# Beacon attention and a two-layer MLP in one kernel: the first sequence cut at query 240, up weights loaded in quarters

## The chip, the cores and the metric

The kernel runs on one core of a Trainium2 chip. The metric is the device time of one execution in microseconds (us), lower is better. The engines are named as in the profile: PE multiplies matrices (PEld loads its weights), ACT (ScalarE) and DVE (VectorE) work on tiles in on-chip memory, POOL (GpSimd) too, and SP issues DMAs; ACT and POOL issue DMAs as well.

## The reference

Eight sequences of 576 tokens, 8 heads of 64 each, with 16 beacon keys and values in front that every query sees:

```python
scores = scale * np.matmul(q, k_all.transpose(0, 1, 3, 2))
causal[:, Nb:] = np.triu(np.ones((S, S), dtype=bool), k=1)
scores = np.where(causal, -1000000000.0, scores)
a = np.exp(scores - scores.max(-1, keepdims=True))
a /= a.sum(-1, keepdims=True) + 1e-09
attn_out = np.matmul(a, v_all)
x = attn_out.transpose(0, 2, 1, 3).reshape(B * S, H * D)
h = x @ w_in
out = np.maximum(0.01 * h, h) @ w_out
```

q, k and v are 8 x 8 x 576 x 64, w_in is 512 x 2048, w_out 2048 x 512, and out 4608 x 512, all float32.

## The kernel before

**Units.** A group is one pair of heads of one sequence; sequence b has groups 4b to 4b+3, so there are 32. Tokens go through the MLP in 9 chunks of 512. Matmuls take bfloat16.

**Attention of one group.** Keys lie along partitions in five blocks (128, 128, 128, 128, 80 rows, the first with the 16 beacon keys). `score` multiplies key blocks with queries into a PSUM tile of two heads x 512 columns (two such buffers), and ACT takes the exponential of the whole tile into `aT` (line 276 in the first eight groups, 329 and 333 later). POOL then zeroes the triangles above the diagonal (`triangle`, line 289). `value` multiplies `aT` with the values, which carry a column of ones, in two halves (query tiles 0 to 2, then 3 and 4; line 359); DVE takes the reciprocal of the row sums (388) and multiplies (389). For groups 0 to 3 PE turns the result and DVE or ACT copies it into `xT` (405, 410).

**The MLP.** An up block (`moe1`, run by `up`) is 4 matmuls of 128 x 512 (line 442) for one of 16 slices of the hidden width, and a Prelu on ACT (450). It needs the tokens of all four groups of a sequence. Chunk 0 goes down through plain matmuls (`moe2_plain`, line 519, 16 down blocks); later chunks use sums of weights and of tokens to save products (line 544).

**Order.** The program is scheduled by hand: every engine runs its instructions in the order in which the code issues them. The prologue is written as strings of steps for `run` (lines 927 to 938): s scores, m masks, v values, q and k turn a group's queries and keys, x finishes a group, u an up block, d a down block, l and V and N load, i and o load up and down weights, w and W are matmuls on a blank tile whose result nothing reads. The prologue computes groups 0 to 7, chunk 0's up blocks and its first down blocks; from group 8 on a list of events with due times fills in up and down blocks between scores and values.

**Loads.** All loads of q, k, v and weights are issued by POOL and cast from float32 on the way, except for the keys of group 0, which SP loads as float32 and ACT and DVE cast (928, 929). Loads for groups 0 to 7 put 9 consecutive rows of a head in one partition (`load_qk`, 158), and PE turns them (`t_q`, 243; copies at 249). Up weights come in two halves (131), down weights in two halves (137).

## Time and profile before

| what | value |
|---|---|
| median of 3 runs | 324.78 us (323.4 to 324.84) |
| span of the profiled execution | 323.8 us |
| PE busy | 314.3 us (97%), 3468 matmuls |
| ACT, DVE, POOL busy | 203.8, 168.0, 184.3 us |
| first exponential | 7.74 us |
| first up matmul | 26.07 us |
| scores of sequence 2 begin | 61.15 us |

The records give one profiled execution, known by its span from the first to the last instruction; the median of the runs is 1.0 us above it. PE's busy time counts pipelined matmuls with their latency, so a busy PE need not be at its peak: an up matmul is recorded as 379 ns long while 537 of them keep PE busy for 116.5 us, 217 ns each. In the first 18 us part of PE's busy time is matmuls on the blank tile.

### The profile page before, as it was taken

What the parts mean: (1) busy time and instruction counts of PE and PEld (TensorE: products, weight loads), DVE (VectorE), ACT (ScalarE), POOL (GpSimd) and SP (SyncE); (2) the same over time, 40 slices, a digit from 0 to 9 for tenths busy, and PEclk for the clock granted to TensorE, in tenths of its full rate; (3) what the DMA queues carried; (4) which work ended last, traced back from release to release, by engine and by line L of the source; (5) the groups of instructions that cost most, each with busy time, mean ns of one, the idle gap of its engine ahead of it and who ended that gap; (6) DMA issues with size and microseconds to landing.
All of it is one profiled execution on the core that took longest, in us unless ns stands there. A gap on an engine that the chain in (4) does not pass through costs nothing.

```text
span 323.8 us, 8701 instructions
## 1 busy us (share of the span) xinstructions
PE 314.3 (97%) x3468; PEld 219.1 (68%) x3494; DVE 168.0 (52%) x341; ACT 203.8 (63%) x346; POOL 184.3 (57%) x354
## 2 busy tenths in 40 slices
PE   7999999999999999999999999999999999999995
PEld 4575555444588557855788888656875697688784
DVE  3464245508255244444443454525464689577954
ACT  4968962387855786478746874687458547455510
POOL 8895868999996787659875977666221000000000
PEclk9999999999999999999999999999999999999999
DMA  8999999999999999999999999999222100200123
GB/s 137 129 189 192 124 214 140 169 177 188 135 152 160 216 138 129 114 186 97 141 176 174 99 143 119 188 128 129 44 81 82 26 2 32 75 25 2 65 67 130
DMA packets 155256, 39.78 MB, mean 123 GB/s; under 512 B 142368, under 2 KB 152480, under 8 KB 155216
## 3 DMA queue, kind: packets, MB, share of 16 engines
q0 software_dynamic: 99824, 18.54, 91.1%
q1 hardware_dynamic: 55120, 20.62, 38.3%
q8 instruction: 27, 0.44, 0.6%
q14 instruction: 13, 0.11, 0.1%
q10 hardware_dynamic: 272, 0.07, 0.1%
HBM read 37.22 MB, written 9.44 MB: 144 GB/s over the span
## 4 chain that ended last, share of the span: by engine, by line
PE 72%; DMA 14%; POOL 9%; ACT 3%; issue 1%; DVE 0%; POOLq 0%; ACTq 0%; SPq 0%
PE acc L442 24%; PE acc L544 19%; PE sc L544 11%; PE av L359 6%; PE sc L314 5%; PE acc L663 5%; DMA w_out_sb<-in_moe_w_out_dram 4%; DMA gsum<-in_k_dram 4%; POOL aT L289 3%; DMA k_nat<-in_k_dram 3%; DMA v_aug<-in_v_dram 2%; ACT aT L333 2%; DMA kT<-k_nat 2%; POOL gsum L158 1%; POOL v_aug L214 1%
## 5 line engine op out<-in xcount | busy, mean ns | idle before, releaser
L442 PE MATMUL acc<-xT,w_in_sb 128*128 128x512 bf16 (+1 forms) x537 | 116.5, 354 | 1.5 <-ACT aT L329 0.3
L450 ACT ACTIVATE gT<-acc 128x512 bf16<-128x512 f32 x124 | 70.8, 623 | 33.1 <-PE acc L442 32.6
L289 POOL TENSOR_SCALAR_AFFINE_SELECT aT<-aT 128x256 bf16<-128x256 bf16 (+2 forms) x160 | 59.7, 403 | 51.4 <-ACT aT L329 31.5
L442 PEld LDWEIGHTS <-w_in_sb 128*128 128x128 bf16 x560 | 51.7, 98 | 43.9 <-issue 2.9
L544 PEld LDWEIGHTS <-gT 128*128 128x128 bf16 x512 | 48.7, 98 | 7.7 <-issue 1.8
L333 ACT ACTIVATE aT<-sc 128x1024 bf16<-128x1024 f32 (+3 forms) x64 | 51.7, 892 | 0.0
L329 ACT ACTIVATE aT<-sc 128x512 bf16<-128x512 f32 (+3 forms) x64 | 29.0, 520 | 27.8 <-PE sc L314 27.8
L388 DVE RECIPROCAL rec<-av 128x6 f32<-128x6 f32 (+1 forms) x64 | 12.0, 187 | 65.0 <-PE av L359 64.4
L359 PEld LDWEIGHTS <-aT 128*128 128x128 bf16 (+1 forms) x960 | 36.9, 98 | 9.2 <-issue 1.4
L544 PEld LDWEIGHTS <-gsum 128*128 128x128 bf16 x384 | 36.5, 98 | 6.5 <-issue 0.4
L359 PE MATMUL av<-v_aug,aT 128*128 128x65 bf16 (+1 forms) x960 | 39.8, 194 | 0.8 <-DMA v_aug<-in_v_dram 0.4
L214 POOL DMA_DIRECT2D v_aug<-in_v_dram x40 | 34.1, 856 | 4.2 <-DMA w_in_sb<-in_moe_w_in_dram 3.8
L171 POOL DMA_DIRECT2D k_nat<-in_k_dram x48 | 34.8, 730 | 0.9 <-DMA w_out_sb<-in_moe_w_out_dram 0.3
L171 POOL DMA_DIRECT2D q_nat<-in_q_dram x48 | 34.8, 729 | 0.6 <-issue 0.4
L389 DVE TENSOR_TENSOR x_nat<-av,rec 128x384 bf16<-128x384 f32 (+1 forms) x64 | 31.4, 491 | 2.2
L544 PE MATMUL acc<-w_out_sb,gT 128*128 128x256 bf16 x240 | 28.9, 273 | 0.4 <-ACT gT L450 0.4
L276 ACT ACTIVATE aT<-sc 128x1024 bf16<-128x1024 f32 (+3 forms) x32 | 26.0, 874 | 4.7 <-PE sc L267 2.5
L314 PE MATMUL sc<-qT,kT 64*128 64x80 bf16 (+22 forms) x384 | 22.2, 250 | 0.3
L314 PEld LDWEIGHTS <-kT 64*128 64x128 bf16 x384 | 12.8, 94 | 11.2 <-issue 7.6
L544 PE MATMUL acc<-w_sum,gsum 128*128 128x256 bf16 x160 | 20.1, 273 | 0.0
L575 ACT COPY p<-acc 128x512 f32<-128x512 f32 x15 | 9.1, 604 | 16.8 <-PE acc L544 16.8
L785 DVE TENSOR_TENSOR gsum<-gT 128x1024 bf16<-128x1024 bf16 x16 | 11.0, 688 | 15.7 <-ACT gT L450 15.7
(95 smaller groups left out, 339.0 us busy)
## 6 DMA issues: line engine op xcount, KB each, us to landing
out_dram<-p SPq DMA_DIRECT2D x26, 256.0 KB, 3.2
q_nat<-in_q_dram POOLq DMA_DIRECT2D x48, 72.0 KB, 5.5
k_nat<-in_k_dram POOLq DMA_DIRECT2D x48, 72.0 KB, 5.3
v_aug<-in_v_dram POOLq DMA_DIRECT2D x24, 128.0 KB, 6.5
w_in_sb<-in_moe_w_in_dram POOLq DMA_DIRECT2D x2, 1024.0 KB, 12.4
w_out_sb<-in_moe_w_out_dram POOLq DMA_DIRECT2D x2, 1024.0 KB, 12.1
out_dram<-u SPq DMA_DIRECT2D x8, 256.0 KB, 2.7
gsum<-in_q_dram POOLq DMA_DIRECT2D x8, 144.0 KB, 7.1
```

The lines of the kernel that those rows point to most:

```text
L171: nc.gpsimd.dma_start(out=t[:, :, par], in_=(q, k)[which][b, 2 * hp + par].rearrange("(t p) d -> p t d", p=NR),)
L214: nc.gpsimd.dma_start(out=dst[lo : ROWS[c], c, :, 0:D], in_=v[b, :, OFF[c] : OFF[c] + n].rearrange("h p d -> p h d"),)
L276: nc.scalar.activation(out=aT[:, :, c0 : c0 + w], in_=sc[:, :, 0:w], func=AF.Exp, scale=0.125)
L289: nc.gpsimd.affine_select(out=view, in_=view, compare_op=ALU.is_ge, fill=0.0, base=128 - n if lo == 0 else 0, channel_multiplier=-1, patte ...
L314: nc.tensor.matmul(out=(sc[par] if apart else sc[:, par])[:, at : at + b - a], lhsT=kT[ps_, c * 128 : (c + 1) * 128], rhs=qT[ps_, q0 : q0 ...
L329: nc.scalar.activation(out=probs[g][:, par, lo:hi], in_=sc[par][:, at : at + hi - lo], func=AF.Exp, scale=0.125)
L333: nc.scalar.activation(out=probs[g][:, :, lo:hi], in_=sc[:, :, at : at + hi - lo], func=AF.Exp, scale=0.125)
L359: nc.tensor.matmul(out=avv[:, n, 0 : D + 1], lhsT=aT[0 : ROWS[c], par, a0 : a0 + 128], rhs=va[0 : ROWS[c], c, 2 * hp + par, :], start=(c = ...
L389: nc.vector.tensor_tensor(out=x_nat[:, t0:t1].rearrange("p t e d -> p (t e) d"), in0=avv[:, :, 0:D], in1=rec[:, n0:n1, None].to_broadcast( ...
L442: nc.tensor.matmul(out=acc[:, lo:hi], lhsT=w_in_cols(fc, j), rhs=xT[:, j, x0 : x0 + hi - lo], start=(j == 0), stop=(j == NJ - 1), skip_gro ...
L450: nc.scalar.activation(out=gT[i][:, fc, :], in_=acc, func=AF.Prelu, alpha=0.01)
L544: nc.tensor.matmul(out=acc[:, lo : lo + HD], lhsT=left(i, n, fc, tile), rhs=right(n, fc), start=(lo == 0 and fc == 0), stop=(fc == HF - 1) ...
```

## The change

Sequence 0 (groups 0 to 3) is taken in two parts. Part a is queries 0 to 239 against the first two key blocks; part b is queries 240 to 575 against all five.

- Rows 0 to 255 of q and k of the four groups come in eight float32 loads (`load_a`), keys on SP's queue and queries on ACT's; ACT, DVE and POOL cast them for two groups at a time (`cast_a`), PE turns two groups with 8 transposes, and four copies put them in place (`turn_a`). Rows 256 to 575 come in eight casting loads on POOL (`load_b`) and are turned by `turn_b`, four copies of 320 columns for each two groups.
- `score_a` puts a group's part a in one tile of 368 columns a head; `score_b` puts part b in three tiles (512, 512, 272 columns).
- The masks of part a of groups 0 and 1 are multiplications with a triangle of ones on DVE (`mask_a`); the others stay on POOL.
- `value` is cut after query tile 1; the turn into `xT` is cut there too.
- `moe1_early` computes two of the 16 slices of chunk 0 for tokens 0 to 239 and takes them through one Prelu; tokens 240 to 511 follow in `moe1`, 272 columns wide. The early half of eight slices stands inside part b, that of the other eight among the scores of group 5.
- Up weights come in four loads.
- The blank matmuls are 9 at the start; the other 50 are taken out.

The new order on ACT. Before, from the third score tile of group 2 (`aT2`) to the first up block; `gT` is the hidden layer:

```order
L276 ACTIVATE aT2_92<-sc_409 128x2x416
L276 ACTIVATE aT2_92<-sc_458 128x2x288
L276 ACTIVATE aT3_93<-sc_472 128x2x512
L276 ACTIVATE aT3_93<-sc_494 128x2x464
L276 ACTIVATE aT3_93<-sc_518 128x2x416
L276 ACTIVATE aT3_93<-sc_551 128x2x288
L410 COPY xT_86<-tp_557 128x576
L249 COPY kT_94<-tp_635 128x576
L410 COPY xT_86<-tp_693 128x576
L276 ACTIVATE aT0_90<-sc_700 128x2x512
L276 ACTIVATE aT0_90<-sc_704 128x2x464
L450 ACTIVATE gT_721<-acc_722 128x512
```

Now, from the part a exponential of group 2; L346 is part a, L369 part b, L549 the Prelu of `moe1_early`, L509 the copy into `xT`:

```order
L346 ACTIVATE aT2_93<-sc_211 128x2x368
L346 ACTIVATE aT3_94<-sc_228 128x2x368
L369 ACTIVATE aT0_91<-sc_287 128x2x512
L509 COPY xT_87<-tp_315 128x240
L369 ACTIVATE aT0_91<-sc_319 128x2x512
L509 COPY xT_87<-tp_327 128x240
L549 ACTIVATE gT_334<-acc_335 128x2x240
L369 ACTIVATE aT0_91<-sc_345 128x2x272
L549 ACTIVATE gT_334<-acc_352 128x2x240
L369 ACTIVATE aT1_92<-sc_363 128x2x512
L369 ACTIVATE aT1_92<-sc_397 128x2x512
L369 ACTIVATE aT1_92<-sc_406 128x2x272
```

The first Prelu stood behind all exponentials of groups 0 to 3 and two of group 4; now it stands between the second and the third part b exponential of group 0.

The new order on DVE, ahead of the first up matmuls. Before, the casts and copies that turn keys and queries (`k_nat`, `tp`), then the first values:

```order
L929 CAST k_nat0_97<-gsum2_96 64x9x64
L249 COPY kT_94<-tp_202 128x117
L249 COPY kT_94<-tp_202 128x459
L249 COPY qT_230<-tp_231 128x576
L249 COPY kT_94<-tp_259 128x576
L249 COPY qT_295<-tp_296 128x576
L249 COPY kT_94<-tp_320 128x576
L249 COPY qT_386<-tp_387 128x576
L249 COPY kT_94<-tp_415 128x576
L388 RECIPROCAL rec_441<-av_362 128x6
```

Now, from the triangle masks of group 1 (L377); L483 and L484 normalise values, L223 copies part b's keys and queries:

```order
L377 TENSOR_TENSOR aT1_92<-aT1_92,tri_81 128x2x112
L377 TENSOR_TENSOR aT1_92<-aT1_92,tri_81 128x2x128
L483 RECIPROCAL rec_218<-av_219 128x4
L484 TENSOR_TENSOR x_nat_217<-av_219,rec_218 128x256
L483 RECIPROCAL rec_235<-av_236 128x4
L484 TENSOR_TENSOR x_nat_234<-av_236,rec_235 128x256
L509 COPY xT_87<-tp_245 128x240
L223 COPY kT_95<-tp_257 128x320 x2
L223 COPY qT_171<-tp_270 128x320
L223 COPY qT_174<-tp_270 128x320
L509 COPY xT_87<-tp_283 128x240
L483 RECIPROCAL rec_294<-av_295 128x4
```

The masks, the normalisation of groups 0 and 1 and a copy into `xT` now stand ahead of the copies that part b's scores need.

The new order on POOL around the down weights. Before, from the masks of group 4 (`aT0`); `bk_raw` are the beacon keys:

```order
L289 AFFINE_SELECT aT0_90<-aT0_90 128x2x128 x3
L289 AFFINE_SELECT aT0_90<-aT0_90 80x2x80
L137 DMA w_out_sb_84<-in_moe_w_out_dram 128x4x1024
L185 DMA bk_raw_98<-in_beacon_k_dram 128x6x64
L289 AFFINE_SELECT aT1_91<-aT1_91 128x2x112
L289 AFFINE_SELECT aT1_91<-aT1_91 128x2x128 x3
L289 AFFINE_SELECT aT1_91<-aT1_91 80x2x80
L137 DMA w_out_sb_84<-in_moe_w_out_dram 128x4x1024
L289 AFFINE_SELECT aT2_92<-aT2_92 128x2x112
L171 DMA q_nat_963<-in_q_dram 96x6x64 x2
```

Now, from the last values of sequence 1; `aT2` and `aT3` belong to groups 6 and 7:

```order
L275 DMA v_aug1_90<-in_v_dram 128x8x64 x3
L275 DMA v_aug1_90<-in_v_dram 80x8x64
L396 AFFINE_SELECT aT2_93<-aT2_93 128x2x112
L150 DMA w_out_sb_85<-in_moe_w_out_dram 128x4x1024
L396 AFFINE_SELECT aT2_93<-aT2_93 128x2x128 x3
L396 AFFINE_SELECT aT2_93<-aT2_93 80x2x80
L246 DMA bk_raw_100<-in_beacon_k_dram 128x6x64
L396 AFFINE_SELECT aT3_94<-aT3_94 128x2x112
L150 DMA w_out_sb_85<-in_moe_w_out_dram 128x4x1024
L396 AFFINE_SELECT aT3_94<-aT3_94 128x2x128 x3
```

The two loads of down weights moved from behind the masks of groups 4 and 5 to behind the first masks of groups 6 and 7.

The diff, cut to its core:

```diff
+    QA, RA, RB = 240, 4, 5
+    LATE0 = 368
+    LATE = [0, 336, 672, 1008, 1216, 1296]
...
     def load_w_in(i):
-        n = DF // 2
-        loaded["w_in", i] = nc.gpsimd.dma_start(
-            out=w_in_sb[i], in_=w_in_r[:, :, i * n : (i + 1) * n]
+        n = DF // 4
+        half, at = i // 2, i % 2 * n
+        nc.gpsimd.dma_start(
+            out=w_in_sb[half][:, :, at : at + n], in_=w_in_r[:, :, i * n : (i + 1) * n]
         )
...
+    def load_a(g, which, eng):
+        _, hp, grp, rows = where(g)
+        eng.dma_start(
+            out=raw_a[grp][rows, which],
+            in_=(q, k)[which][0, 2 * hp : 2 * hp + 2, 0 : RA * RP].rearrange("h (p i) d -> p h i d", i=RA),
+        )
...
+    def turn_a(grp, copies):
+        n, w = RA * RP, RA * 128
+        ps = ps_one.tile([128, 1024], BF16, name="tp", tag="one")
...
+        for e in range(2):
+            for which in (1, 0):
+                copies[which * 2 + e](
+                    out=operand(2 * grp + e, which)[:, 0:n].rearrange("c (p i) -> c p i", i=RA),
+                    in_=ps[:, which * w : (which + 1) * w].rearrange("c (i e p) -> c e p i", i=RA, e=2)[:, e],
+                )
...
+    def score_a(g):
+        qT, kT = qk[g]
+        aT = probs[g] = a_bufs[g % NA]
+        sc = ps_sc.tile([128, 2, 512], FP32, name="sc", tag="sc")
+        for c in range(2):
+            w = QA - OFF[c]
...
+        nc.scalar.activation(
+            out=aT[:, :, 0:LATE0], in_=sc[:, :, 0:LATE0], func=AF.Exp, scale=0.125
+        )
...
+    def score_b(g, n):
+        qT, kT = qk[g]
+        lo, hi = n * 512, min(LATE[NKB], n * 512 + 512)
...
+        nc.scalar.activation(
+            out=probs[g][:, :, LATE0 + lo : LATE0 + hi], in_=sc[:, :, 0 : hi - lo], func=AF.Exp, scale=0.125
+        )
...
+    def mask_a(g, eng):
+        for lo, n in ((0, 112), (QA, 128)):
+            if eng == 0:
+                view = probs[g][:, :, lo : lo + n]
+                nc.vector.tensor_tensor(
+                    out=view, in0=view, in1=tri[:, None, 128 - n :].to_broadcast([128, 2, n]), op=ALU.mult
+                )
+            else:
+                triangle(probs[g], lo, n, 128)
...
+    def moe1_early(n):
+        if 0 not in gT:
+            gT[0] = gpool.tile([128, NF, 512], BF16, name="gT")
+        acc = ps_one.tile([128, 512], FP32, name="acc", tag="one")
+        for f in range(2):
+            moe1_part(acc[:, f * QA :], 2 * n + f, 0, QA, first=f == 0)
+        nc.scalar.activation(
+            out=gT[0][:, 2 * n : 2 * n + 2, 0:QA],
+            in_=acc[:, 0 : 2 * QA].rearrange("p (f t) -> p f t", f=2),
+            func=AF.Prelu,
+            alpha=0.01,
+        )
...
+        if i == 0:
+            moe1_part(acc, fc, QA, 512)
+            nc.scalar.activation(out=gT[0][:, fc, QA:], in_=acc[:, 0 : 512 - QA], func=AF.Prelu, alpha=0.01)
+            return
...
-        load_first_keys()
+        for g in range(NPAIR):
+            load_a(g, 1, nc.sync)
+        load_a(0, 0, nc.scalar)
         load_beacon_k(0, 2, nc.scalar)
+        for g in range(1, NPAIR):
+            load_a(g, 0, nc.scalar)
...
-        unused(13, 256)
+        unused(9, 256)
...
-        run("q0.1 k0 w2.384 s0.0 m0.0 w3.256 s0.1 q1 s0.2 m0.1 k1 s0.3 m0.2")
...
+        run("g0.1.1 g0.0.0 A0.0.0.1.1 a0 a1 g1.1.2 g1.0.0 j0.0 A1.0.0.1.0 j1.0 a2 f0.0 a3 f1.0 z0.0.0 j2.1 j3.1 L2.0 L2.1 L3.0 L3.1 B0.0.0.0.0 z1.0.0 b0.0 f2.0 f3.0 z2.1.0 b0.1 z3.1.0")
...
```

In the new strings g casts part a, A and B turn parts a and b, a and b score them, j and n mask them, f takes values, z turns a part into `xT`, c runs `moe1_early` and L loads part b.

210 lines of the change are left out of this document (140 added, 70 removed).

## The prediction

> **What bounds the kernel now.** I read the page first, then PE's waits by stretch, then the timeline of the first 62 us, then the groups by form there. The page:
>
> ```profile
> span 323.8 us, 8701 instructions
> ...
> PEclk9999999999999999999999999999999999999999
> ```
>
> The waits of the tensor engine (PE) from 61 us, where the scores of sequence 2 begin, to the end (us in total, times, longest):
>
> ```profile
> PE acc L544 <- ACT gT L450: 0.4, 2, 0.2
> PE acc L442 <- ACT aT L329: 0.3, 1, 0.3
> PE acc L519 <- issue: 0.2, 1, 0.2
> PE av L359 <- ACT gT L450: 0.2, 1, 0.2
> ```
>
> They are 1.1 us of 263: from there PE is the limit, and what it still has to do is the same before and after. So the change is worth what it does to the moment at which PE has the prologue behind it. The prologue in order of time (start, duration, engine, work, idle time before it):
>
> ```profile
> 0.81 1.21 SPq L165 DMA_DIRECT2D gsum<-in_k_dram  x2
> ...
> 1.07 2.95 PE L825 MATMUL av<-blank 128*128 128x256 bf16 x13 [1.07 <-DVE blank L917]
> ...
> 3.77 0.67 ACT L928 CAST k_nat<-gsum 64x576 bf16<-64x576 f32 x1 [0.28 <-DMA gsum<-in_k_dram]
> ...
> 5.62 0.74 DVE L929 CAST k_nat<-gsum 64x576 bf16<-64x576 f32 x1 [0.87 <-DMA gsum<-in_k_dram]
> ...
> 5.91 0.47 PE L243 MATMUL tp<-ident,gsum 64*64 64x64 bf16 x18 [0.83 <-DMA gsum<-in_q_dram]
> ...
> 7.31 0.39 PE L267 MATMUL sc<-qT,kT 64*128 64x512 bf16 x2
> ...
> 7.74 8.89 ACT L276 ACTIVATE aT<-sc 128x1024 bf16<-128x1024 f32 x11 [0.68 <-PE sc L267]
> ...
> 20.56 1.54 ACT L276 ACTIVATE aT<-sc 128x832 bf16<-128x832 f32 x2 [0.42 <-PE sc L267]
> ...
> 26.07 1.90 PE L442 MATMUL acc<-xT,w_in_sb 128*128 128x512 bf16 x7
> ```
>
> From 7.74 to 22.1 us ScalarE (ACT) runs the exponentials of the first four groups almost without a gap; PE looks busy then because blank matmuls fill it. The first up matmul starts at 26.07, when the four groups stand in xT. I call that moment T.
>
> **The change part by part.** Means by form in the first 62 us (behind the bar: busy us, mean ns, idle us):
>
> ```profile
> L450 ACT ACTIVATE gT<-acc 128x512 bf16<-128x512 f32 x16 | 9.2, 606 | 3.2 <-PE acc L442 2.8 <-PE tp L243 0.2
> ...
> L276 ACT ACTIVATE aT<-sc 128x1024 bf16<-128x1024 f32 x8 | 8.2, 1023 | 1.0 <-PE sc L267 1.0
> ...
> L276 ACT ACTIVATE aT<-sc 128x576 bf16<-128x576 f32 x8 | 5.3, 662 | 1.1 <-PE sc L267 1.0
> ...
> L389 DVE TENSOR_TENSOR x_nat<-av,rec 128x384 bf16<-128x384 f32 x8 | 4.5, 557 | 0.3
> ...
> L389 DVE TENSOR_TENSOR x_nat<-av,rec 128x256 bf16<-128x256 f32 x8 | 3.4, 424 | 0.3
> ...
> L410 DVE COPY xT<-tp 128x576 bf16<-128x576 bf16 x5 | 2.3, 455 | 3.8 <-PE tp L405 3.8
> ...
> L388 DVE RECIPROCAL rec<-av 128x4 f32<-128x4 f32 x8 | 1.4, 179 | 2.7 <-PE av L359 2.7
> ...
> L410 ACT COPY xT<-tp 128x576 bf16<-128x576 bf16 x2 | 1.3, 636 | 0.7 <-PE tp L405 0.7
> ...
> L249 DVE COPY kT<-tp 128x459 bf16<-128x459 bf16 x1 | 0.6, 625 | 0.0
> ...
> L249 DVE COPY kT<-tp 128x117 bf16<-128x117 bf16 x1 | 0.3, 283 | 0.6 <-PE tp L238 0.6
> ```
>
> And from the page, over the whole run:
>
> ```profile
> L289 POOL TENSOR_SCALAR_AFFINE_SELECT aT<-aT 128x256 bf16<-128x256 bf16 (+2 forms) x160 | 59.7, 403 | 51.4 <-ACT aT L329 31.5
> ...
> L276 ACT ACTIVATE aT<-sc 128x1024 bf16<-128x1024 f32 (+3 forms) x32 | 26.0, 874 | 4.7 <-PE sc L267 2.5
> ...
> L785 DVE TENSOR_TENSOR gsum<-gT 128x1024 bf16<-128x1024 bf16 x16 | 11.0, 688 | 15.7 <-ACT gT L450 15.7
> ```
>
> *Start.* The first 256 rows of q and k of all four groups now come in eight loads on SP's and ACT's queues. DVE and ACT can cast the first pair of groups once two key and two query loads have landed. Before, one load was cast at 3.77 and the next at 5.62; I take 5.2, nearer the later one, because the second query load stands third on ACT's queue; bounds 3.8 and 6.6. A cast takes .66 (744 ns x 512/576), eight transposes about .45 (18 small ones took .47), a DVE copy of 256 columns .42 (1.0 ns a column between the two L249 rows), the scores .45 with the hand-over (.39 and a gap). First exponential at 7.2, against 7.74.
>
> The Trainium skill ("DMA: Bandwidth & Descriptors", section "Issuing engines are not separate DMA queues") says that loads issued from different engines run on the same 16 DMA engines and that several issuers save issue time alone. By it the start would lie at the late bound, 1.4 us more. Two loads issued .6 apart here (0.81, two in 1.21) were cast 1.85 apart, which agrees.
>
> *ACT's work.* An exponential costs .81 ns a column and .2 fixed (from 1023 and 662 ns). Part a is 4 x 736 columns at .79, part b 4 x (1.02 + 1.02 + .64): 13.9 us, as much as now (16 x 874 ns = 14.0). New in this stretch are four Prelus of 480 columns at .58 (from 606 ns), one key copy and two xT copies at about .4 each (from 636 ns): 17.4 us in all, so 24.6 if ACT never idles.
>
> *ACT's new idle time.* First, part b of group 0 needs its q and k turned, and those copies stand on DVE behind all of part a: two casts 1.3, five copies 2.1, four masks by the new triangle 1.1 (at L785's .67 ns a column, 240 of 480 columns each pair and a fixed part; at most 2), two normalisations 1.2 (179 + 424 each), one xT copy .25, then three of the four 320-column copies at .49: 7.4 us from 5.2, so 12.6, and with the scores 13.1. ACT is through part a at 10.8, thus 2.3 idle; behind the waiting exponential stand the xT copies of groups 2 and 3, on which the first up matmuls wait. Second, those matmuls (c0) need the first 240 tokens of all four groups. DVE still has one copy, one xT copy and two normalisations (1.94, so 14.6); ACT copies the last xT piece after its next exponential, until 16.1; eight matmuls take 1.1 with their drain, and c0's Prelu stands ahead of the next exponential on ACT, as c0 stands ahead of its scores on PE: 1.3 idle. Together 3.6; bounds 0 (two score buffers cover it) and 5.5. The last exponential ends at 28.2.
>
> *Tail.* Two masks on GpSimd .8, the last value matmuls .4, DVE .74 (557 + about 180), transposes .35, copy .3: 2.6. T is 30.8, 4.7 later than 26.1. Before, 4.0 us lay between the last exponential and T, but PE turned and scored group 4 in them, which is priced next.
>
> *What is credited.* PE's prices, the first two from the groups, the others from the timeline:
>
> ```profile
> L442 PE MATMUL acc<-xT,w_in_sb 128*128 128x512 bf16 (+1 forms) x537 | 116.5, 354 | 1.5 <-ACT aT L329 0.3
> ...
> L544 PE MATMUL acc<-w_out_sb,gT 128*128 128x256 bf16 x240 | 28.9, 273 | 0.4 <-ACT gT L450 0.4
> ```
>
> ```profile
> 25.16 0.59 PE L267 MATMUL sc<-qT,kT 64*128 64x512 bf16 x4
> ...
> 27.90 0.48 PE L267 MATMUL sc<-qT,kT 64*128 64x336 bf16 x8
> 28.30 0.75 PE L243 MATMUL tp<-ident,gsum 64*64 64x64 bf16 x36
> ```
>
> 512 columns take 217 ns (116.5/537), 256 take 120 (28.9/240): halves cost more than a whole. By that slope 240 take about 115 and 272 about 128, so cutting chunk 0 adds 64 x 26 ns = 1.7 us to PE, .4 of it before T. Done before T: 8 of 16 blocks of 240 tokens, worth 32 x 217 x 240/512 = 3.25 us. Moved behind T: q and k of group 4 and two score tiles, .75 + .59 less their drains, 1.0. After T ACT has six Prelus at .41 and four exponentials for group 4, 6.0 us; PE has six blocks at .51 and .75 + 1.07, 4.9: 1.1 lost. Sum -3.25 + 1.3 + 1.0 + 1.1 = about +.1. The blank matmuls taken out (all but 9) lay in PE's idle time: nothing.
>
> *Loads.* On GpSimd the down weights go out behind the masks of groups 6 and 7 instead of 4 and 5, and part b of groups 2 and 3 behind masks that wait for ACT's fourth exponential.
>
> ```profile
> 39.96 0.77 POOL L137 DMA_DIRECT2D w_out_sb<-in_moe_w_out_dram  x1
> ...
> 53.70 3.61 PE L519 MATMUL acc<-w_out_sb,gT 128*128 128x512 bf16 x15
> ...
> 61.15 0.85 PE L314 MATMUL sc<-qT,kT 64*128 64x512 bf16 x12
> ```
>
> ```profile
> DMA to landing us min/median/max: 10.6/12.1/13.7
> ```
>
> The second half (39.96) landed 13.7 later and PE started on it at 53.70. Now it is issued near 52, and PE reaches it near 58. If it lands in 6 us, because less is queued ahead, nothing is lost; that is taken. At the shortest landing shown, 10.6, it costs about 4, in the range. The up weights in quarters let c0 start on a quarter of the bytes; their landing is hidden behind the DVE chain, and if it were not, c0 alone would wait.
>
> **Sum.** 4.7 + .1 = 4.8 on the profiled span of 323.8, so 328.6. The median of the runs shown, 324.78, lies 1.0 above that span, so the forecast is 329.5.
>
> **Rivals.** *Dense start (faster).* Part a lands at 3.8, the first exponential starts at 5.8, ACT never idles, the tail shrinks to 1.9: T = 25.1, 1.0 earlier, and group 4 is no longer ACT's (1.1): -2.0 with the .1, 322.7. For it: the blanks show how little PE has to do there, and two score buffers cover short waits. Against it: the 7.4 us on DVE alone. With the other terms as summed it decides from T below 24.4.
>
> *Loads decide (same).* PE met the down weights as they landed (53.7). If the bytes pace the prologue, both kernels reach sequence 2 together: 324.8. For it: that meeting. Against it: PE's own work fills 26 to 61.
>
> *Down weights late (slower still).* The same chain plus 3.5: 333.0. It decides if the second half lands more than 6 us after its issue.
>
> *Cold PE (slower still).* The 13 blank matmuls at the start took 2.95 us, 227 ns for 256 columns against 120 later, so PE begins at half pace. With blanks gone from 3 to 17 us, the chained transposes, scores, values and c0, c1 could run so: 2 us of them doubled, 331.5. Against it: the granted clock reads 9 in every slice of the page and shows no such state.
>
> The Trainium skill ("TensorE: Matmul & The Clock Gate", Part 1) says that PE's clock is halved until about 3.4 us of sustained matmuls and again after an idle window, and its Part 4 that transposes don't count as activity. By it this rival would hold, at 331.5.
>
> **How the numbers follow.** A measurement of this kernel tells about 0.5% (1.6 us) from no change. Forecast .52 (its own range 327 to 332.5), dense start .16, loads decide .14, down weights late .10, cold PE .08. So slower .52 + .10 + .08 = .70, same .14, faster .16. The range takes in dense start and late weights with a later start: 322.5 to 334.0.
>
> **What would show it.** In the changed kernel's timeline: first exponential near 7.2; ACT idle about 2 us after the fourth 736-column exponential, ended by scores that wait for a DVE copy; c0 near 16.1; the first 272-column matmul near 31; PE's waits for the down weights under 1 us; first scores of sequence 2 near 67, with two more down blocks done. Wrong would be T below 27, or PE with fewer idle gaps before T than now, or a join that waits for loads.

## The result, and the profile after

The changed kernel takes 350.31 us in the median of 4 runs (348.82 to 350.58), the kernel before 324.18 beside it: a ratio of 1.079 (95% interval 1.076 to 1.082). The profiled execution spans 348.6 us instead of 323.8, so 24.8 us of loss are there to be found. The forecast was 329.5 (322.5 to 334.0): the sign was right, the size five times too small.

The page of the changed kernel, with the row of the granted clock and the one of the DMA engines (one digit for each of 40 slices of 8.7 us, 9 is full):

```profile
span 348.6 us, 8681 instructions
...
PE   3688795959999999999999999999999999999995
...
PEclk9999999678999999999999999999999999999999
DMA  9899749999999999999999999999911200200113
```

PE is not steadily full before the end of slice 10 (87 us), the granted clock falls in slices 8 to 10 (61 to 87 us), and the DMA engines, which read 9 there in the kernel before, have gaps in slices 5 and 6 (35 to 52 us). Behind slice 10 PE is full again. PE's timeline around the start of sequence 2, which began at 61.15 before:

```profile
69.07 1.89 PE L648 MATMUL acc<-w_out_sb,gT 128*128 128x512 bf16 x8
74.18 0.85 PE L255 MATMUL tp<-ident,bk 128*64 128x128 bf16 x12 [3.21 <-POOL bk L249]
75.32 1.87 PE L648 MATMUL acc<-w_out_sb,gT 128*128 128x512 bf16 x4 [0.29 <-DMA w_out_sb<-in_moe_w_out_dram]
...
79.11 5.07 PE L648 MATMUL acc<-w_out_sb,gT 128*128 128x512 bf16 x20
...
84.28 3.62 PE L648 MATMUL acc<-w_out_sb,gT 128*128 128x512 bf16 x16
87.83 0.84 PE L421 MATMUL sc<-qT,kT 64*128 64x512 bf16 x12
```

The scores of sequence 2 (line 421 now) start 26.7 us later. There, 48 plain down matmuls are done (12 blocks) and not 40, as the change has it; at 217 ns the 8 are worth 1.7. Net 25.0: the whole loss lies ahead of this row. It has two parts of about equal size.

**Up to T.** ACT's timeline from the first exponential on, and the one row of DVE that decides its start (columns as in the prediction's timeline):

```profile
8.96 0.43 DVE L194 CAST q_nat<-gsum 128x512 bf16<-128x512 f32 x1 [1.75 <-DMA gsum<-in_q_dram]
```

```profile
11.51 1.64 ACT L346 ACTIVATE aT<-sc 128x736 bf16<-128x736 f32 x2 [0.18 <-PE sc L338]
...
18.98 1.02 ACT L369 ACTIVATE aT<-sc 128x1024 bf16<-128x1024 f32 x1 [2.58 <-PE sc L361]
...
23.61 0.57 ACT L549 ACTIVATE gT<-acc 128x480 bf16<-128x480 f32 x1 [1.25 <-PE acc L534]
...
25.66 0.57 ACT L549 ACTIVATE gT<-acc 128x480 bf16<-128x480 f32 x1 [0.97 <-PE acc L534]
```

PE in the same stretch:

```profile
16.20 1.28 PE L218 MATMUL tp<-ident,gsum 128*64 128x128 bf16 x20
...
23.85 1.78 PE L534 MATMUL acc<-xT,w_in_sb 128*128 128x240 bf16 x8
...
25.92 0.75 PE L218 MATMUL tp<-ident,gsum 128*64 128x128 bf16 x20
...
31.46 0.99 PE L534 MATMUL acc<-xT,w_in_sb 128*128 128x240 bf16 x8 [0.55 <-DMA w_in_sb<-in_moe_w_in_dram]
...
38.16 1.32 PE L534 MATMUL acc<-xT,w_in_sb 128*128 128x272 bf16 x8
```

The first exponential comes at 11.51 (7.74 before), and T, the first matmul of 272 columns, at 38.16 (26.07 before): 12.1 later, of which 3.8 is the start and 8.3 the stretch from the first exponential to T (26.65 against 18.33). Until about 25.7 PE needs 1.28 us for 20 transposes and 1.78 for eight 240-column matmuls; later the same work takes 0.75 and 0.99.

**From T to sequence 2.** 49.7 us, less the two down blocks 48.0, against 35.1 before: 12.9 more. PE's waits in that stretch, and the rows of the stretch by windows (busy time of PE, then of PEld, DVE, ACT and POOL, then the granted clock):

```profile
PE tp L255 <- POOL bk L249: 3.2, 1, 3.2
PE av L464 <- DMA v_aug<-in_v_dram: 2.6, 2, 1.5
```

```profile
59.81:66.64 6.83, 6.34 (x85) 4.11 (x85) 2.90 (x7) 2.14 (x4) 0.77 (x3) 0.50 1.24 188
73.47:80.29 6.82, 5.82 (x54) 3.85 (x55) 2.44 (x7) 0.00 (x0) 6.82 (x14) 0.50 1.87 132
```

With 0.3 for the down weights, PE waits 6.1 us for loads and for GpSimd's cast. And in two windows of 6.8 us, each beginning within or at the end of such waits, the granted clock is 0.50 while PE is busy 6.34 and 5.82 us: half of that, 6.1, is lost if all of it would have run in half the time. Why the loads are late stands in GpSimd's timeline:

```profile
66.14 0.37 POOL L396 TENSOR_SCALAR_AFFINE_SELECT aT<-aT 128x224 bf16<-128x224 bf16 x1 [6.07 <-ACT aT L326]
66.47 0.77 POOL L150 DMA_DIRECT2D w_out_sb<-in_moe_w_out_dram  x1
...
70.71 1.47 POOL L232 DMA_DIRECT2D q_nat<-in_q_dram  x2 [0.63 <-issue]
72.17 1.44 POOL L232 DMA_DIRECT2D k_nat<-in_k_dram  x2
73.61 0.52 POOL L249 CAST bk<-bk_raw 128x384 bf16<-128x384 f32 x1
```

GpSimd stands 6.07 us at a mask of group 7, whose exponential is late; the second half of the down weights is behind it, and is issued at 66.47 where the prediction had 52.

### The profile page after: what moved, and what is told of

Its sections match the earlier page's. It is cut to its first block, busy times and chain, and to the rows that moved or that the text cites. A ratio compares the mean times of both kernels' runs of the same rounds, so it can differ in the third digit from the quotient of the medians.

```text
span 348.6 us, 8681 instructions
## 1 busy us (share of the span) xinstructions
PE 323.2 (93%) x3453; PEld 226.2 (65%) x3453; DVE 169.7 (49%) x357; ACT 203.9 (59%) x355; POOL 187.2 (54%) x355
## 4 chain that ended last, share of the span: by engine, by line
PE 79%; DMA 7%; ACT 5%; POOL 3%; issue 2%; DVE 2%; ACTq 0%; POOLq 0%; DVEq 0%
PE acc L571 25%; PE acc L673 18%; PE sc L673 11%; PE av L464 7%; PE sc L421 6%; PE acc L792 4%; PE acc L648 4%; DMA w_out_sb<-in_moe_w_out_dram 3%; PE acc L534 2%; ACT aT L440 2%; DMA gsum<-in_q_dram 2%; DMA w_in_sb<-in_moe_w_in_dram 2%; DMA v_aug<-in_v_dram 1%; POOL v_aug L275 1%; ACT aT L326 1%
## 5 line engine op out<-in xcount | busy, mean ns | idle before, releaser
L571 PE MATMUL acc<-xT,w_in_sb 128*128 128x512 bf16 (+1 forms) x496 | 102.0, 352 | 0.0
L579 ACT ACTIVATE gT<-acc 128x512 bf16<-128x512 f32 x108 | 61.5, 630 | 28.8 <-PE acc L571 28.6
L571 PEld LDWEIGHTS <-w_in_sb 128*128 128x128 bf16 x496 | 46.1, 98 | 37.4 <-issue 1.7
L440 ACT ACTIVATE aT<-sc 128x1024 bf16<-128x1024 f32 (+3 forms) x64 | 51.8, 895 | 0.0
L483 DVE RECIPROCAL rec<-av 128x6 f32<-128x6 f32 (+1 forms) x64 | 12.0, 187 | 75.3 <-PE av L464 74.8
L464 PEld LDWEIGHTS <-aT 128*128 128x128 bf16 (+1 forms) x960 | 38.4, 101 | 12.1 <-issue 5.1
L464 PE MATMUL av<-v_aug,aT 128*128 128x65 bf16 (+1 forms) x960 | 41.6, 199 | 2.6 <-DMA v_aug<-in_v_dram 2.6
L484 DVE TENSOR_TENSOR x_nat<-av,rec 128x384 bf16<-128x384 f32 (+1 forms) x64 | 31.4, 491 | 2.2
L534 PE MATMUL acc<-xT,w_in_sb 128*128 128x272 bf16 (+1 forms) x128 | 20.3, 300 | 1.1 <-DMA w_in_sb<-in_moe_w_in_dram 0.5
L421 PEld LDWEIGHTS <-kT 64*128 64x128 bf16 x384 | 12.9, 94 | 10.9 <-issue 7.8
L914 DVE TENSOR_TENSOR gsum<-gT 128x1024 bf16<-128x1024 bf16 x16 | 11.0, 689 | 16.4 <-ACT gT L579 11.7
```

The costliest lines, as they stand in the source:

```text
L421: nc.tensor.matmul(out=(sc[par] if apart else sc[:, par])[:, at : at + b - a], lhsT=kT[ps_, c * 128 : (c + 1) * 128], rhs=qT[ps_, q0 : q0 ...
L440: nc.scalar.activation(out=probs[g][:, :, lo:hi], in_=sc[:, :, at : at + hi - lo], func=AF.Exp, scale=0.125)
L464: nc.tensor.matmul(out=avv[:, n, 0 : D + 1], lhsT=aT[0 : ROWS[c], par, a0 : a0 + 128], rhs=va[0 : ROWS[c], c, 2 * hp + par, :], start=(c = ...
L484: nc.vector.tensor_tensor(out=x_nat[:, t0:t1].rearrange("p t e d -> p (t e) d"), in0=avv[:, :, 0:D], in1=rec[:, n0:n1, None].to_broadcast( ...
L534: nc.tensor.matmul(out=out[:, 0 : hi - lo], lhsT=w_in_cols(fc, j), rhs=xT[:, j, lo:hi], start=(first and j == 0), stop=(j == NJ - 1), skip ...
L571: nc.tensor.matmul(out=acc[:, lo:hi], lhsT=w_in_cols(fc, j), rhs=xT[:, j, x0 : x0 + hi - lo], start=(j == 0), stop=(j == NJ - 1), skip_gro ...
```

## The experiments

Theory 1: PE runs at half pace for want of the blanks. Theory 2: loads issued late, and the clock that goes with the waits. Theory 3, formed on the way: PE's own sequence, with its hand-overs, is the chain up to T. The rival to all was the prediction's own account (ACT's work and DVE's queue). Spans are of one profiled execution, which lay 1.7 us below the median for the changed kernel, 2.8 below for the one with early loads and 0.6 above for "blanks, first half whole", so small differences go by the ratios. Kernels that share the beginning of the changed one reach the first exponential anywhere between 10.77 and 12.41, so T is best compared by its distance from it, T - exp. All times in us; "exp" is the first exponential, "seq. 2" the first scores of sequence 2.

| kernel | exp | T | T - exp | seq. 2 | span | ratio to before (95%) |
|---|---|---|---|---|---|---|
| before | 7.74 | 26.07 | 18.3 | 61.15 | 323.8 | 1 |
| changed | 11.51 | 38.16 | 26.7 | 87.83 | 348.6 | 1.079 (1.076 to 1.082) |
| blanks back | 11.01 | 37.17 | 26.2 | 87.05 | 347.8 | 1.082 (1.078 to 1.086) |
| cast early | 11.39 | 38.54 | 27.2 | 88.03 | 348.8 | 1.081 (1.078 to 1.083) |
| blanks in the late waits | 11.44 | 38.32 | 26.9 | 85.34 | 347.8 | 1.073 (1.068 to 1.077) |
| **early loads** | 10.99 | 37.48 | 26.5 | 75.83 | 340.1 | 1.055 (1.053 to 1.058) |
| the same, and: | | | | | | |
| blanks, too many | 14.48 | 40.54 | 26.1 | 78.90 | 344.7 | 1.064 (1.059 to 1.069) |
| first pair's bytes first | 10.32 | 38.90 | 28.6 | 77.25 | 340.5 | 1.059 (1.053 to 1.064) |
| early groups behind T | 10.77 | 35.04 | 24.3 | 76.44 | 341.9 | 1.058 (1.053 to 1.062) |
| short exponentials | 16.22 | 41.94 | 25.7 | 80.28 | 344.8 | 1.067 (1.064 to 1.071) |
| two DVE masks less | 12.41 | 39.04 | 26.6 | 77.41 | 341.1 | 1.059 (1.055 to 1.062) |
| part b and quarter 2 early | 11.04 | 37.62 | 26.6 | 75.96 | 340.6 | 1.058 (1.054 to 1.061) |
| blanks, few | 10.78 | 37.09 | 26.3 | 75.45 | 339.1 | 1.049 (1.044 to 1.054) |
| blanks, first half whole | 11.29 | 36.26 | 25.0 | 74.62 | 342.5 | 1.050 (1.044 to 1.056) |
| before, without blanks | 8.11 | 27.88 | 19.8 | 61.63 | 324.6 | 1.004 (1.000 to 1.007) |
| before, chunk 0 cut | 7.54 | 25.45 | 17.9 | 61.85 | 325.3 | 1.003 (1.000 to 1.006) |

In "early groups behind T" and "before, chunk 0 cut" T is the first 240-column matmul.

### Late loads

*Early loads.* The loads of groups 6 and 7 (what the first words of the expectation mean), the values of sequence 1, the later beacon keys and the down weights go out in one piece once chunk 0's up weights are issued, and GpSimd's cast of the beacon keys moves ahead of the last two masks of group 7:

```diff
-        run("u u q4 k4 u s4.0 u s4.1 m4.0 u s4.2 u s4.3 m4.1 l6.0 l6.1 m4.2 q5 k5 u u c4 s5.0 c5 s5.1 m5.0 l7.0 l7.1 c6 s5.2 c7 s5.3 m5.1 V1.0 m5.2 V1.1 V1.2 V1.3 V1.4 u u q6 k6 u s6.0 u s6.1 m6.0 o0 u s6.2 s6.3 m6.1 m6.2")
+        run("l6.0 l6.1 l7.0 l7.1 V1.0 V1.1 V1.2 V1.3 V1.4 o0")
         load_beacon_k(2, B, nc.gpsimd)
+        run("o1 u u q4 k4 u s4.0 u s4.1 m4.0 u s4.2 u s4.3 m4.1 m4.2 q5 k5 u u c4 s5.0 c5 s5.1 m5.0 c6 s5.2 c7 s5.3 m5.1 m5.2 u u q6 k6 u s6.0 u s6.1 m6.0 u s6.2 s6.3 m6.1 m6.2")
-        run("v4.0 v4.1 y4 u q7 k7 u s7.0 v5.0 s7.1 m7.0 o1 v5.1 u s7.2 s7.3 m7.1 m7.2 N8.0 N8.1")
+        run("v4.0 v4.1 y4 u q7 k7 u s7.0 v5.0 s7.1 m7.0 v5.1 u s7.2 s7.3")
         cast_beacon_k(2, B, nc.gpsimd.tensor_copy)
-        run("v6.0 v6.1 x5 N9.0 T8 d d")
+        run("m7.1 m7.2 N8.0 N8.1 v6.0 v6.1 x5 N9.0 T8 d d")
```

> The changed kernel, with the issues of both halves of the down weights' first quarter loads, the values of sequence 1, the later beacon keys and both down-weight halves put on GpSimd ahead of the masks of group 4, as soon as chunk 0's up weights are issued, and the cast of the beacon keys ahead of the last two masks of group 7. Theory 2 (late issue: PE waits for V1, the beacon keys and the second down half at 57 to 61 and 71 to 75 us, and loses the clock for 6.8 us after each): the 2.6 + 3.2 + 0.3 us of waits go, and the two half-clock stretches with them (up to 3.4 us each), so 9 to 12 us less: 337 to 340 us, ratio 1.040 to 1.052. Rival (PE is late anyway, and the waits only show up elsewhere, at masks or exponentials): less than 3 us, ratio above 1.070.

Its page and PE's waits from 38 to 88 us:

```profile
span 340.1 us, 8661 instructions
...
PEclk9999999999999999999999999999999999999999
```

```profile
PE sc L317 <- DVE kT L302: 2.0, 3, 0.7
PE sc L421 <- DMA kT<-k_nat: 1.4, 1, 1.4
```

The waits for values, beacon keys and down weights are gone and the clock is full. Sequence 2 starts 12.0 earlier, 0.7 of it ahead of T; the span is 8.5 shorter, as 3.5 come back later. Of these, 1.4 are the new wait for turned keys of sequence 2 and 1.7 a new wait for values at 117.66. By the ratios the gain is 7.7 us. Theory 2 holds, a little under its size (1.040 to 1.052 was expected): a third of the loss.

*Cast early.* The changed kernel with `cast_beacon_k(2, B, ...)` ahead of `m7.1 m7.2 N8.0 N8.1`, all else as it was.

> The changed kernel with one edit: GpSimd casts the later beacon keys ahead of the last two masks of group 7 and of eight DMA issues, instead of behind them. Theory 2a (PE's 3.2 us wait at 71 us belongs to the second half of the down weights as much as to this cast, since that half lands at 75.3): the wait changes its name and stays, gain under 1 us, ratio 1.076 to 1.079. Rival (it is the place of the cast in GpSimd's queue alone): the wait goes and so does the half clock after it, 4 to 6 us less, ratio 1.060 to 1.067.

PE at that place:

```profile
71.39 0.53 PE L255 MATMUL tp<-ident,bk 128*64 128x128 bf16 x12
75.29 1.86 PE L648 MATMUL acc<-w_out_sb,gT 128*128 128x512 bf16 x4 [3.38 <-DMA w_out_sb<-in_moe_w_out_dram]
```

The wait only changed its name, from 3.21 for the cast to 3.38 for the down weights; nothing is gained. Behind the wait that the profile named, another of the same length was hidden.

*Blanks in the late waits.* The changed kernel with 10 blank matmuls of 512 columns ahead of and between `v4.0 v4.1`, and 20 ahead of the later beacon transposes.

> The changed kernel with blank matmuls (10 and 20 of 512 columns) put where PE waits at 57 to 60 and at 71 to 74 us; all loads stay late, so the waits themselves stay. If the clock that is lost after each wait is a cost of its own (two stretches of 6.8 us at half clock): the granted clock stays full, and 4 to 6.5 us are gained, ratio 1.059 to 1.067. If the waits alone cost: the ratio stays at 1.079 or rises by the blanks' time.

The granted clock is full there (1.00 from 60 to 80, against 0.67), sequence 2 starts 2.5 earlier, the ratio falls by 0.6 points: about 2 us, under the 4 to 6.5 expected. Part is given back: the blanks outlast the waits (the beacon transposes start at 74.70 instead of 74.18), and the profiled execution lost the clock elsewhere (0.72 from 38 to 44, where the changed kernel has 1.00), which cost it some 0.8 behind T. The clock is a cost of its own, and by these runs the smaller share of the two.

### The clock at the start

*Blanks back.* In the changed kernel, 13 blanks at the start instead of 9, then `w13.256`, `w8.384` and 14 short `w` steps of 2 to 4 blanks each between the steps of the first 18 us.

> The changed kernel, with blank matmuls put back into its first 18 us (13 at the start and some 30 small ones between the steps); nothing else moves. Theory 1 (PE runs at half pace until 25.7 us because the blanks are gone, and the chain waits for PE in places): the granted clock is full from about 4 us, the 20 transposes of part b take about 0.75 us instead of 1.28, c1's eight matmuls 1.0 instead of 1.8, and the first 272-column matmul comes 2 to 4 us earlier than 38.2; ratio to before 1.068 to 1.073 instead of 1.079. Rival (the chain is set by DVE, ACT and the loads, PE's pace is hidden, as the prediction had it): the clock is full but that matmul stays within 0.7 us of 38.2 and the ratio at 1.079.

PE's timeline of it:

```profile
16.64 0.75 PE L218 MATMUL tp<-ident,gsum 128*64 128x128 bf16 x20
...
23.05 0.99 PE L534 MATMUL acc<-xT,w_in_sb 128*128 128x240 bf16 x8
...
30.47 0.99 PE L534 MATMUL acc<-xT,w_in_sb 128*128 128x240 bf16 x8 [1.14 <-DMA w_in_sb<-in_moe_w_in_dram]
```

PE is at full pace (0.75, 0.99) and c1 is through 1.6 us earlier (24.0 against 25.6), but T gains only 1.0 (37.17), half of it ahead of the first exponential, and the ratio doesn't fall. c2 now waits 1.14 for the second quarter of the up weights, not 0.55, and behind T PE's waits for values grow from 2.6 to 3.3. Theory 1 is right about the pace, but its 2 to 4 us at T don't come.

*Before, without blanks.* The same cause alone, on the kernel before: all blanks behind the first 9 taken out.

> The kernel before, without its blank matmuls behind the first 9. Theory of the prediction (blanks lie in PE's idle time and hide nothing): no change, ratio 0.997 to 1.003. Rival (they keep the clock up): transposes and scores of groups 0 to 3 run at half pace for their first 10 to 20 us, the first up matmul comes 1 to 3 us later than 26.1, and the ratio is 1.003 to 1.010.

T comes at 27.88, 1.8 later, sequence 2 at 61.63, 0.5 later, and the ratio is 1.004 (1.000 to 1.007), 1.2 us. The blanks in the kernel before were worth something, if little; "nothing" was wrong.

*Blanks with early loads.* The early loads with the same blanks as in "blanks back" ("blanks, too many" in the table):

> The kernel with the early loads (on record as 340.1 us of span, 37.48 for the first 272-column matmul), and with the blank matmuls back in its first 18 us. With late loads the blanks moved that matmul from 38.16 to 37.17 only and gained nothing at the end; if that was because the late loads took the gain back, the kernel now gains what PE's pace is worth: the same 1 us, at most 2 (c0 and c1 at 1.0 instead of 1.8 us each), so a ratio of 1.050 to 1.052 against 1.055. Rival (the quarters of the up weights and the part b loads, whose landing doesn't depend on PE, take over): within 0.3 us, ratio 1.054 to 1.057.

It is slower than its parent, the kernel with early loads, by 4.6 us of span, for a reason of its own. PE at the start of it and, behind it, of "blanks back":

```profile
6.67 0.42 PE L255 MATMUL tp<-ident,bk 128*64 128x128 bf16 x4 [2.65 <-ACT bk L249]
7.03 5.51 PE L954 MATMUL av<-blank 128*128 128x256 bf16 x21
12.33 0.63 PE L204 MATMUL tp<-ident,k_nat 128*128 128x128 bf16 x4
```

```profile
6.04 0.30 PE L255 MATMUL tp<-ident,bk 128*64 128x128 bf16 x4 [2.02 <-ACT bk L249]
6.27 2.89 PE L954 MATMUL av<-blank 128*128 128x256 bf16 x21
```

The beacon keys came 0.6 later, PE waited 2.65 and not 2.02, it ran at half pace behind that, and 21 blanks (13 of 256 columns, 8 of 384) that took 5.51 us stood ahead of the first key transposes, which moved the first exponential to 14.48. So it leaves the question open, and two kernels without that fault tell it apart. *Blanks, few*: 26 at the start (until the beacon keys), 8 behind them, the short ones as before. *Blanks, first half whole*: besides, `i1` right behind `i0`, and `L2`, `L3`, `V0.2` to `V0.4` ahead of `j2.1 j3.1`, so that no transfer stands in the way.

> The kernel with the early loads and blank matmuls, this time so few at the start (26 until the beacon keys land, 8 behind them) that none stands ahead of the first key transposes when those can run. Theory 3 (PE's own sequence is the chain from the first exponential to the first 272-column matmul, 26.5 us in the parent, and half of it runs at half pace): that stretch shrinks by 1 to 3 us, less where the second quarter of the up weights, whose issue waits for c1's last matmul, then holds c2. Rival (hand-overs from PE to DVE and back set it, at any clock): it shrinks by less than 0.5 us, and the ratio stays within 0.003 of the parent's 1.055.

> The same kernel with the first two quarters of the up weights issued together ahead of everything that waits, and the loads of part b of groups 2 and 3 and of three value blocks ahead of GpSimd's two masks. Neither the clock nor a transfer then holds PE between the first exponential and the first 272-column matmul. Theory 3: the stretch of 26.5 us shrinks by 2 to 4 us, and the end comes 2 to 4 us earlier than in the parent, ratio 1.043 to 1.050. Rival (hand-overs): by less than 1 us, ratio 1.052 or more.

The stretch from the first exponential to T shrinks from 26.5 to 26.3 with the clock alone and to 25.0 with the transfer out of the way too. The ratios go to 1.049 and 1.050, 2 us below the parent's 1.055, with intervals that overlap its own. In the first kernel the stretch goes as the rival said, the ratio does not; in the second the ratio just meets theory 3, and the 1.5 of the stretch lie between the theory's 2 to 4 and the rival's 1.

The blanks themselves blur this test. The profile's view of the chain of waits goes back from T, at each step to what released the work; its first line gives each line's share. For the second kernel, from 11.3 to 36.5 us:

```profile
by line: PE av L464 16.0%; PE acc L534 13.3%; PE av L954 11.4%; PE sc L361 10.1%; DVE kT L223 7.1%; DVE x_nat L484 6.2%; PE tp L503 5.8%; DVE qT L223 4.8%; ACT aT L369 4.0%; PE sc L338 3.7%; DVE qT L207 3.5%; PE tp L218 3.3%; issue 2.6%; AC
```

The blanks (line 954) are 11.4% of it, 2.9 us. Summed over all pieces of this view, PE has 18.4 us of the parent's stretch and 16.4 here, 13.5 of them real work. So half pace makes some 4.9 us of the parent's stretch, by this estimate, and the blanks that cure it take 2.9 back. How much of the 4.9 would arrive at full pace without blanks, no run shows. DVE's pieces are 6.0 us in both.

### What sets the stretch from the first exponential to T

*Short exponentials.* Part b's exponentials on a quarter of their columns, 6.1 us less for ACT (DVE fills the rest beforehand, which delays the start to 16.22; only the stretch is compared):

```diff
+        n = (hi - lo) // 4
         nc.scalar.activation(
-            out=probs[g][:, :, LATE0 + lo : LATE0 + hi], in_=sc[:, :, 0 : hi - lo], func=AF.Exp, scale=0.125
+            out=probs[g][:, :, LATE0 + lo : LATE0 + lo + n], in_=sc[:, :, 0:n], func=AF.Exp, scale=0.125
         )
```

> The kernel with the early loads, with the exponentials of part b of sequence 0 on the first quarter of their columns only (the other three quarters of the weights are left at one), so ACT has 8 x (1.02 - 0.41) + 4 x (0.62 - 0.31) = 6.1 us less to do there; scores, masks, values and all hand-overs stay. Theory (ACT's work plus fixed waits set the moment at which the first 272-column matmul starts, as the prediction's sum had it): that moment comes 5 to 6 us earlier than 37.5, ratio about 1.037 to 1.041. Rival (the chain is made of hand-overs between PE, DVE and ACT and of transfers, and shorter exponentials only turn into longer waits): it comes less than 3 us earlier, ratio 1.047 or more.

ACT's and PE's timelines:

```profile
16.22 1.65 ACT L348 ACTIVATE aT<-sc 128x736 bf16<-128x736 f32 x2 [0.18 <-PE sc L340]
...
23.70 0.38 ACT L372 ACTIVATE aT<-sc 128x256 bf16<-128x256 f32 x1 [2.59 <-PE sc L363]
```

```profile
41.94 1.32 PE L537 MATMUL acc<-xT,w_in_sb 128*128 128x272 bf16 x8
```

The stretch is 25.7 instead of 26.5. Of 6.1 us taken from ACT, 0.8 arrive; c2 waits 0.66 for the second quarter of the up weights here, so without that at most 0.7 more would. ACT's work is not the chain. What the chain is made of is read from the view of the waits, for the early-loads kernel from 11 to 38 us:

```profile
by line: PE av L464 17.8%; PE acc L534 17.1%; PE sc L361 13.5%; DVE kT L223 6.6%; PE tp L503 6.3%; DVE x_nat L484 5.8%; PE sc L338 5.2%; PE tp L218 5.1%; DVE qT L223 4.5%; ACT aT L369 3.8%; PE tp L204 3.6%; DVE qT L207 3.2%; DVE rec L483 2.
```

Seven lines of PE hold 69% of it and DVE's over 20%; ACT's part b exponentials have 3.8%. PE's instructions stand in one order, transposes, scores, values and early up blocks of the four groups in turn, and DVE's copies come between. In the changed kernel itself the same view, from 11.5 to 38 us, takes another way:

```profile
by line: DMA w_in_sb<-in_moe_w_in_dram 20.7%; issue 14.6%; POOL v_aug L275 9.5%; POOL gsum L185 8.8%; PE av L464 8.3%; PE acc L534 6.9%; PE sc L338 5.4%; POOL aT L396 4.3%; DVE x_nat L484 4.3%; PE tp L204 3.7%; DVE qT L207 3.3%; ACT aT L346
```

It goes back through c2's wait of 0.55 for the second quarter to GpSimd's issues and masks. This rival path is worth little: with early loads c2 doesn't wait, and the stretch is 26.5 instead of 26.7.

*Two DVE masks less.* Steps `j0.0` and `j1.0` taken out, so the triangles of part a of groups 0 and 1 are not zeroed.

> The kernel with the early loads, without the two multiplications by the triangle that DVE does for groups 0 and 1 in part a (those triangles are left out of the computation), 0.96 us of DVE's work ahead of the copies of part b. Theory (ACT's 2.6 us wait before its first part b exponential is DVE's queue): the wait falls by 0.7 to 1.0 and the first 272-column matmul comes 0.5 to 1.0 earlier. Rival (the wait belongs to the part b transposes on PE or to their loads): the wait stays within 0.3.

```profile
12.41 1.64 ACT L346 ACTIVATE aT<-sc 128x736 bf16<-128x736 f32 x2 [0.17 <-PE sc L338]
...
19.88 1.02 ACT L369 ACTIVATE aT<-sc 128x1024 bf16<-128x1024 f32 x1 [2.58 <-PE sc L361]
```

The wait stays at 2.58, and 7.47 lie between these rows as in the changed kernel (11.51 to 18.98). So these 0.96 us of DVE's queue are not what ACT waits for, as the rival said. Of its two causes the rows leave PE's order: the part b transposes (16.20 in the changed kernel) have no wait before them and stand behind the scores, values and x transposes of part a, and behind them come DVE's copies.

*Part b and quarter 2 early.* `L2`, `L3`, `V0.2` to `V0.4` and `i1` ahead of GpSimd's masks `j2.1 j3.1`.

> The kernel with the early loads, with the loads of part b of groups 2 and 3, of three value blocks and of the second quarter of the up weights issued on GpSimd ahead of its two masks of part a (from about 10 us on instead of 16.6 to 25.4). Theory (the DMA engines run empty between 14 and 17 and again between 25 and 28 us, and all that is queued behind is late by as much): the first 272-column matmul comes 0.5 to 1.5 us earlier and the end 1 to 3 us, ratio 1.046 to 1.052. Rival (those transfers are in time already; PE waits for none of them in the parent): nothing before that matmul moves by more than 0.3 us, ratio 1.054 to 1.057.

```profile
21.75 1.58 PE L534 MATMUL acc<-xT,w_in_sb 128*128 128x240 bf16 x7 [0.67 <-DMA w_in_sb<-in_moe_w_in_dram]
```

T stays (37.62), as the rival said. The quarters aren't independent as the program has them: with `i1` issued ahead of c0, c0 waits 0.67 for its landing, and with `i1` behind c1, as in the change, GpSimd waits 3.34 for c1's matmuls before it issues it:

```profile
25.93 0.77 POOL L144 DMA_DIRECT2D w_in_sb<-in_moe_w_in_dram  x1 [3.34 <-PE acc L534]
```

*First pair's bytes first.* Queries of group 1 ahead of the beacon keys on ACT's queue, beacon keys cast and turned behind the first casts, and `V0.0` to `i0` behind GpSimd's cast of the second key pair.

> The kernel with the early loads, and with the bytes of the first two groups put first: the queries of group 1 ahead of the beacon keys on ACT's queue, the beacon keys cast and turned behind the first pair's casts, and all casting loads (values, part b, up weights) issued on GpSimd behind its cast of the second key pair instead of from 1.7 us on. Theory (the prediction's start failed because the four loads of the first pair share the DMA engines with what was issued beside them): first exponential at 8.5 to 9.2 instead of 11.0, everything up to the first 272-column matmul earlier by about 2, and 2 us at the end, ratio 1.047 to 1.050. Rival (the start is not what sets the chain: values and part b land later and hold it): the first exponential is earlier, that matmul within 0.7 us of 37.5, ratio 1.053 or more.

```profile
10.32 1.46 ACT L346 ACTIVATE aT<-sc 128x736 bf16<-128x736 f32 x2 [1.42 <-PE sc L338]
```

The second query load lands early enough for its cast at 6.54 instead of 8.46, but the first exponential gains 0.7 only (the scores now wait for the beacon columns), and T comes 1.4 later, at 38.90: PE now waits 1.18 for values and 0.70 for the keys of part b, which land later. The rival is right, and T is even worse than it said; this order of the loads doesn't buy the start.

*Early groups behind T.* c0 to c3 from their places to behind `x3.2`.

> The kernel with the early loads, with the first four early groups of chunk 0 (two up blocks of 240 tokens each, and their Prelus) taken from between the exponentials to the place behind the last x copy of sequence 0; everything else as it was. Theory (they lengthen the chain on ACT by more than their PE work is worth: four Prelus of 0.57, and waits of 1.25 and 0.97 for c0 and c1 at half pace): the first 272-column or 240-column matmul of the up weights behind the last copy comes 3.5 to 5 us earlier than 37.5, four groups of 1.0 are done there instead, and the end moves by -1 to +0.5 us, ratio 1.052 to 1.057. Rival (PE's spare time in the prologue is worth its full length, as the change intends): the end is 3 to 4 us later, ratio 1.065 or more.

```profile
35.04 4.37 PE L534 MATMUL acc<-xT,w_in_sb 128*128 128x240 bf16 x40
```

The early matmuls, with the first 8 of 272 columns behind them, start at 35.04, 2.4 earlier than T was, less than expected. Span 341.9 against 340.1, ratio 1.058 against 1.055 with intervals that overlap: the four early groups gain 0.8 us by the ratios and 1.8 by the spans, not clear of noise. Part of that may be the clock, for PE ran longer at half pace without them: 24 value matmuls took 1.50 us until 29 and 0.91 later, while the parent had 0.92 from 28.4 on.

### The cut of the up matmuls

In `moe1` of the kernel before, for chunk 0: `for lo, hi in ((0, 240), (240, 512))`.

> The kernel before with chunk 0's up matmuls cut at token 240 and nothing else, 240 + 272 columns in place of 512 (64 matmuls more). The prediction's term: 64 x 26 ns = 1.7 us, ratio 1.0045 to 1.006. Rival (in the changed kernel four matmuls of 272 between scores come every 143 ns and not every 128): 64 x 41 ns = 2.6 us, ratio 1.007 to 1.009. If ACT's Prelus and not PE set the pace there: under 0.5 us.

The ratio is 1.003 (1.000 to 1.006): 0.8 us, with 1.7 inside the interval near its upper end, 2.6 outside it, and the third case, under 0.5, inside it too. PE's rows between the same two score tiles settle the term. In the kernel before, and then with the cut:

```profile
31.34 2.76 PE L442 MATMUL acc<-xT,w_in_sb 128*128 128x512 bf16 x12
```

```profile
31.15 2.79 PE L442 MATMUL acc<-xT,w_in_sb 128*128 128x240 bf16 x24
```

The 12 matmuls of 512 columns take 2.76 us and the 24 of 240 and 272 columns 2.79. For all 64 that is some 0.2 us: the term of 1.7 was too large. The execution also waits 2.09 for keys of sequence 2, which accounts for its later scores (61.85).

## Why the prediction was wrong, step by step

Two steps failed most: the path to T, which ran through PE's own order and pace and not through ACT's work, and the loads behind T, which were put at nothing.

- **Start: failed.** "I take 5.2" for the second query load: it was cast at 8.96, beyond the late bound of 6.6. It stood third on ACT's queue, and beside it values and part b loads were already under way. First exponential 11.51 against 7.2: 4.3 us (3.6 to 5.2 by the other executions with this beginning), 3.8 of them the load. The sentence of the Trainium skill ("DMA: Bandwidth & Descriptors", section "Issuing engines are not separate DMA queues") gave 1.4 of them and pointed the right way: when this load stood second on ACT's queue and the loads beside it were issued later, the cast came at 6.54. Which of the two did it, no run tells.
- **ACT's idle time: right size in one place, wrong cause, too small in all.** 2.3 forecast ahead of part b, 2.58 found; but a DVE queue 0.96 us shorter didn't change it. Around c0 and c1 1.3 was forecast and 2.2 found (1.25 and 0.97).
- **The stretch from the first exponential to T: failed in its account.** Forecast 23.6, found 26.7, so 3.1 short, and built on "ACT's work", which the short exponentials showed off the chain: 0.8 of 6.1. PE, said to have little to do there, is 69% of the chain with early loads, by its own order and at half pace for half the way.
- **T: 30.8 forecast, 38.16 found.** 4.3 start + 3.1 stretch = 7.4.
- **Blanks taken out, "nothing": wrong.** They were worth 1.8 us at T in the kernel before. In the changed one and with early loads, putting them back gained 0.4 to 1.0 at T, with the up weights' second quarter next, and net of the time that the blanks take themselves; half pace makes 4.9 us of the stretch by the estimate above. The rival *cold PE* had the mechanism: 20 transposes 1.28 and not 0.75. Its counter-argument, that the clock row reads 9, was wrong: that row reads 9 in the stretch where the rows above show half pace. The Trainium skill ("TensorE: Matmul & The Clock Gate", Part 1) has PE's clock halved until matmuls have been sustained, and the durations agree with it against the row.
- **Down weights, "in 6 us, nothing is lost": the largest failure.** The landing was mis-sized a little (8.8 us), the issue a lot: 66.47, not 52, as each load stands behind a mask, and the mask behind an exponential that the late T (7.4 of the 14.5) moves with it. PE's waits for values and the half clock from 59.81 on moved it further: with early loads the mask that comes at 66.14 here comes at 61.12. Values and beacon keys moved in the same strings got no term at all. Waits of 6.1 and half clock after them: 12.0 up to sequence 2, 8.5 in the span. The rival *down weights late* had the place and a third of the price.
- **Credits, +.1: too kind.** With early loads T to sequence 2 takes 38.35 - 1.7 = 36.6 against 35.1 before, 1.5 slower. In it PE waits 2.0 for the key copies of groups 4, 6 and 7 on DVE (line 302), which weren't priced; the rest stays open. The cut was overpriced: by the prediction's own slope 240 and 272 columns take 114 and 126 ns, so 1.5 us and not 1.7, and the rows show 0.2. With that the credits would have come to about -1, further from what was found.

Added up on the span: late loads 8.5 (7.7 by the ratios), T with early loads 11.4 later (3.3 start, 8.2 stretch), 1.5 behind T, 3.4 that the early loads give back behind the start of sequence 2, together the 24.8. Shown by a run is the first. Of the stretch 1.5 is shown to be clock and quarter, net of 2.9 of blanks, and it is shown that ACT's work and DVE's two masks aren't the rest. How the rest divides between half pace and single hand-overs is read from the chain of waits and stays open. That the start is a matter of bytes is shown only so far that another order of the same loads doesn't bring T forward. No version came near the kernel before; the best, with few blanks and early loads, is 4.9% (4.4 to 5.4) slower.

## What to carry to other kernels

A wait named in a profile can be the last of several: before pricing its removal, or a move, look at what else its place waits for. A load behind a wait on an in-order queue moves with everything that makes that wait later, so a delay of the front is paid again at each later join; issue loads by need, not between the masks where there is room. And cutting work into parts to start earlier adds hand-overs: count them on the engine that has to do all of them in order, here PE, and at the pace that it has there.
